# Two more outputs of the first token pair by seven products, with their weight preparation moved earlier

## The chip, the cores and the metric

One core of one Trainium2 chip runs the whole kernel. The metric is device time in microseconds (us), the median of several runs. Engines: TensorE (PE; its weight loads are PEld), VectorE (DVE), ScalarE (ACT), GpSimd (POOL) and SyncE (SP, which issues most DMAs).

## The reference, cut to what matters

```python
qn, kn = q / (norm(q, axis=1) + 1e-6), k / (norm(k, axis=1) + 1e-6)   # (6016, 256)
a = softmax(kn.T @ qn / tau)                                         # 256 x 256
x = v @ a
h = x @ w_in;  x = (h * sigmoid(1.702 * h)) @ w_out                  # 256 -> 2048 -> 256
h = x @ w2_in; y = (max(h, 0) + alpha * min(h, 0)) @ w2_out
```

All inputs are float32. The weights arrive as 64-bit numbers, read as pairs of 32-bit words.

## The kernel before

Every float32 operand is split into a high and a low part of the reduced format fp32r, and each product is three matmuls (high·high, high·low, low·high). The attention matrix is folded into the first weight, so that W1I = a · w_in is made on the chip and v goes straight into it. Tokens stand in 12 column blocks of 512 or 448, taken as six pairs per layer. The 2048 hidden channels are eight outputs j = 0 to 7 of 256.

**Two ways for one output.** `direct` takes an output's four units (a unit is 128 channels by one token block) by two products each, eight products or 24 matmuls. `quartet` takes the four units by seven products (Strassen's scheme, 21 matmuls). It needs sums of the tokens, T1 to T4, each with a high and a low part, and sums of the weights, S2 to S4 of that output. Either way the eight products `outs.next()` of the output before, with the second weight, are laid between, 24 matmuls. In the first pair of layer 1 outputs below `STRASSEN` go by `direct`, the others by `quartet`. All other pairs use `quartet` alone.

**The order of work** is written by hand, and each engine gets its instructions in the order in which the program emits them. A *place* is one call of `beside(time)`: `direct` has four an output (one a unit), the quartets of the first pair three. It counts places in `conv.now`, first emits up to `most` ScalarE steps that wait in the list `put_off`, and then VectorE steps until `time` us of stated costs are used up. The candidates are the first step of each kind in `bg` (kind 0: token sums, kind 1: weight sums) and the next step of the converter; the earliest due number goes first, and the converter wins a tie.

**The converter** turns 64-bit weights into high and low parts, one piece of 128 x 512 at a time: `ia[j]` is the inner weight of output j, `ob_[j]` the outer one. ScalarE scales (L138), VectorE does shift, power and rest (L142, L155, L158). Then a piece either takes a ScalarE copy and two more VectorE steps (less, low: L182, L185), or, where `added`, GpSimd issues an accumulating DMA (L162), three places later ScalarE's copy (L151) is asked for, and VectorE splits off the low part (L165, `settle`). The copy asked for goes through `put_off`; the split comes in the place in which the copy has been emitted. One piece in flight is asked for in a place.

**W1I.** `emit_w(j)` makes it for outputs 1 to 3; `emit_pair(j)` for outputs 4, 5 and 6, 7 with twelve matmuls of 512 columns into two PSUM banks (L723), two ScalarE writes of the high parts (L726) and two VectorE writes of the low parts (L727) right behind them. `combine` gives the weight sums S2 to S4: `whole` adds high and low again (L694), `sums_` is four small operations (L699 to L702), then ScalarE's high (L708) and VectorE's low (L705).

Of the kernel before, what the change touches and what calls it, by code (L numbers as in the profile page):

```python
# [8 lines left out]
F32 = mybir.dt.float32  # L9
# [6 lines left out]
P = 128  # L16
# [14 lines left out]
FREE = ((0.7, 2.8, 1.7), (0.0, 0.8, 0.8))  # L31
FIRST = 2.1
AHEAD = 2
QK_PARTS = [1, 3] + [4] * 9 + [2, 2, 2, 1]
TAIL = 12
LOADING = 3
LANDING = 3
STRASSEN = 6
ON_VECTOR = (4, 5, 6, 8)
# [20 lines left out]
def attention_then_two_ffns(ctx: ExitStack, tc: tile.TileContext, q, k, vT, tau, w1i, w1o, w2i, w2o, alpha, outT):  # L60
# [129 lines left out]
    class Converter:  # L190


        STEPS = (("shift", 0.45), ("power", 0.45), ("rest", 0.63), ("less", 0.63), ("low", 0.63))
        ADDED = (("shift", 0.45), ("power", 0.45), ("rest", 0.63))

# [30 lines left out]
        def time(self, piece):  # L226
            if not piece or self.landed():
                return 0.63
            return self.list(piece)[self.at][1]
# [35 lines left out]
        def step(self):  # L265

            if self.waits():
                if not self.open:
                    self.scale(True)
                scalar_work()  # L270
            if not self.next() or self.landed():
                self.settle()
                return 0.63
# [35 lines left out]
        def due(self):  # L309
            return min(x.due for x in self.left())  # L310

# [19 lines left out]
    with tc.manual_schedule():  # L331
# [26 lines left out]
        def outer(j, n=1):  # L358
            def pair():
                return tuple(WO[:, j:j + n, h].rearrange("p q a b -> p q (a b)") if n > 1 else flat(WO[:, j, h]) for h in range(2))  # L360
            return Convert(w1o[:, j * PIECE:(j + n) * PIECE].rearrange("p (a n) -> p a n", a=1), pair, added=j > 3)

# [6 lines left out]
        LAST = 4 * STRASSEN  # L369
        PAIRS = {4: 13, 6: min(21, LAST - 2)}  # L370
        for j, x in ia.items():
# [237 lines left out]

        operands, xin2, combining = {}, [], []  # L610

        class Step:
# [7 lines left out]
            def waits(self):  # L620
                return self.needs in put_off

            def run(self):
                if self.waits():
                    scalar_work()
                self.do()
                if self.then:
                    put_off.append(self.then)

        def prepare(l, p):  # L630
# [20 lines left out]
            def minus(nm, a, b):  # L651
# [4 lines left out]
                ("B11", B11), ("B21", B21), ("T1", None), ("T2", None), ("T3", None), ("T4", None), ("B22", B22))}  # L656
            D = 0.63
            early = [
# [18 lines left out]
            if (l, p) == (0, 0):  # L677
                def last():
                    ops["T4"] = operand()
                    tmp["T4"] = tmp["T2"]  # L680
                    minus("T4", B21, "T2")
                steps = [early[i] for i in (2, 3, 6, 7)] + [late[0], Step(D, None, last, hi["T4"])] + [late[i] for i in (4, 5)]
                for x, due in zip(steps, (4, 4, 4, 4, 3, 3, 3, 3)):
                    x.due = LAST - due
                return steps
            return early, late

        def combine(hi, lo, hi_s, lo_s):

            box = {}  # L690
# [12 lines left out]

            def low():
                nc.vector.tensor_tensor(lo_s(), box["s"], f32(hi_s()), ALU.subtract)  # L705

            def high():
                nc.scalar.copy(hi_s(), box["s"])  # L708

            steps = [Step(0.63, None, whole, kind=1), Step(0.9, None, sums_, high, 1), Step(0.63, high, low, kind=1)]  # L710
            combining.append(steps)
            return steps

        def combine_wi(j):
            return combine(*(WI[:, j, h, :4] for h in range(2)), *(lambda h=h: WI[:, j, h, S1:] for h in range(2)))

        def emit_pair(j):

            conv.need([ia[j], ia[j + 1]])
            for m in range(2):  # L720
# [5 lines left out]
                nc.scalar.activation(hi, src, AF.Copy, scale=rs[:, m:m + 1])  # L726
                nc.vector.scalar_tensor_tensor(lo, src, rs[:, m:m + 1], f32(hi), ALU.mult, ALU.subtract)  # L727

        def emit_w(j):
# [6 lines left out]
            for m in range(2):  # L736
                if j > 1 or m:
                    keep_hi(j, m, pw, m * C)
                    keep_lo(j, m, pw, m * C)

        bg = []
        spare = [0.0]

# [6 lines left out]
        def beside(time, convert=False, place=None, most=None):  # L750

            conv.place()
            now = scalar_work(most)
            late = now if place == 0 else []
# [18 lines left out]
        def finish(steps):  # L773

            while any(s in bg for s in steps):
                s = next(x for x in bg if x in steps) if Convert.deep else bg[0]
                bg.remove(s)
                if s.waits():
                    put_off.remove(s.needs)
                    s.needs()  # L780
# [103 lines left out]
        def direct(j, outs, mid_way):  # L884
# [3 lines left out]
            for i, (f, c) in enumerate((f, c) for f in range(2) for c in range(2)):  # L888
# [11 lines left out]
                mid_way(i)  # L900
                beside(FIRST, most=2 if (j, i) == (STRASSEN - 1, 3) else 3)
                u.low()
                units.append((f, c, u.pair))
            return Outs(0, 0, j, units)

        def quartet(l, p, j, outs, carry):
# [20 lines left out]
            ends = (l, p, j) == (1, NP - 1, NQ - 1)  # L927
            most = 1 if l else 2 if narrow else None
            u11, u22, u21, u12 = (Unit(l, 2 * j + f, c) for f, c in ((0, c0), (1, c1), (1, c0), (0, c1)))
            fork = (l, p, j) != (1, 0, 0)  # L930
            a, b = bank(), bank()
            product(a, j, A11, ops["B11"], n, True, True)
# [20 lines left out]
            if j != 1:  # L953
                beside(FREE[l][0], place=0, most=most)
            if fork:
# [11 lines left out]
            if before:  # L967
                b12.low()
            outs.next()
            product(a, j, S2, ops["T2"], n, False, True)  # L970
            u2 = copy(a)
# [5 lines left out]
            outs.next()  # L977
            beside(FREE[l][1], most=most)
            finish(late[:4])
            product(a, j, S3, ops["T3"], n, False, True)  # L980
            u3 = copy(a)
# [3 lines left out]
            evacuate()  # L985
            beside(FREE[l][2], most=most)
            finish(late)
            u22.act()
            product(a, j, A22, ops["T4"], n, False, True)
# [14 lines left out]
            return Outs(l, p, j, [(0, c0, u11.pair), (1, c1, u22.pair), (1, c0, u21.pair), (0, c1, u12.pair)])  # L1004

        operands[0, 0] = blocks
        conv.ahead = True
# [27 lines left out]
        small = [flat(G), Convert.pool.tile([P, T], F32, tag="top", name="second", bufs=3)]  # L1035
        sums0, pair1 = [], []
        outs, carry = None, []
# [21 lines left out]
        def combining_of(n):  # L1059
            combined[n] = combine_wi(n)  # L1060
            for x in combined[n]:
                x.due = LAST + 3 * ((n or NQ) - STRASSEN) - 1
            bg.extend(combined[n])

        def mid_way(i):
# [5 lines left out]
            for n, due in PAIRS.items():  # L1071
                if at == due:
                    emit_pair(n)
                    for m in (n, n + 1):
                        if m >= STRASSEN:
                            combining_of(m)
            if j == 2 and i == 0:
                nc.sync.dma_start(alpha_sb, alpha)
            if at == LAST - 10:
                sums0.extend(prepare(0, 0))  # L1080
                bg.extend(sums0)
            if at == LAST - 2:
                combining_of(0)
            next_pair()

        for j in range(NQ):
            if j:
                conv.need([ob_[j - 1]])
            if j < STRASSEN:
                outs = direct(j, outs, mid_way)  # L1090
                continue
            finish(combined[j])
            finish(sums0)
            next_pair()
# [152 lines left out]
```

## Time and profile before

| | |
|---|---|
| Median of 3 runs | 1032.64 us (1032.48 to 1032.89) |
| The profiled execution | 1033.06 us, of which the trace's span is 1031.3 us |
| TensorE busy | 1025.7 us of the span, 4634 matmuls, granted clock 1.00 |
| VectorE busy | 750.5 us (73%) |
| ScalarE busy | 758.5 us (74%) |
| GpSimd busy | 38.4 us (4%) |

The span runs from the first to the last instruction. What the profiled execution takes beyond it lies before and after. A busy share is a mean over the whole span; the first pair, which the change is about, runs from about 50 to 141 us.

### The profile page before, as it was taken

The numbers are of one execution on the slowest core, as the hardware profiler recorded it, in microseconds if no ns is written. First come the engines' busy times: TensorE is split into PE (matmuls) and PEld (weight loads), VectorE is DVE, ScalarE is ACT, GpSimd is POOL, SyncE is SP. The second block draws the span as 40 slices with busy tenths as digits, with TensorE's granted clock in tenths as the row PEclk, the third lists the DMA queues.
The fourth block names the chain that finished last, engine by engine and source line by source line (L and its number), as shares of the span: only waits on it lengthen the run. The fifth ranks groups of instructions, "written<-read, shape, count | busy, mean of one in ns | idle before, by whom it ended". The sixth has DMA issues, their size and how long they took to land.

```text
span 1031.3 us, 12536 instructions
## 1 busy us (share of the span) xinstructions
PE 1025.7 (99%) x4634; PEld 865.4 (84%) x4634; DVE 750.5 (73%) x1226; ACT 758.5 (74%) x1273; POOL 38.4 (4%) x50
## 2 busy tenths in 40 slices
PE   9999999999999999999999999999999999999998
PEld 8888888888888888888998888888888888888997
DVE  4788888877778765445637877787877787877766
ACT  6787787778778766666767777777777777867776
POOL 4401000000000000000100000000000000000000
PEclk9999999999999999999999999999999999999999
DMA  9737222224325312003553001001001000000100
GB/s 356 266 106 178 65 74 70 98 80 168 114 89 179 113 41 77 1 1 132 196 168 113 1 21 62 1 21 62 1 21 62 1 18 25 36 0 1 41 1 36
DMA packets 32445, 79.72 MB, mean 77 GB/s; under 512 B 3200, under 2 KB 7808, under 8 KB 32384
## 3 DMA queue, kind: packets, MB, share of 16 engines
q1 hardware_dynamic: 28928, 65.29, 18.3%
q0 software_dynamic: 3456, 13.63, 4.6%
q8 instruction: 36, 0.59, 0.2%
q14 instruction: 25, 0.20, 0.1%
HBM read 52.96 MB, written 23.86 MB: 74 GB/s over the span
## 4 chain that ended last, share of the span: by engine, by line
PE 99%; DMA 0%; SPq 0%; ACT 0%; issue 0%
PE ps_o L814 50%; PE ps_h L785 44%; PE gram L433 4%; PE pw L567 1%; PE pw L723 1%; DMA qk<-in_k 0%; SPq L453 0%; PE nrm L510 0%; ACT s L831 0%; PE bc L532 0%; PE pt L555 0%
## 5 line engine op out<-in xcount | busy, mean ns | idle before, releaser
L814 PE MATMUL ps_o<-ghi,wo 128*128 128x512 f32 (+1 forms) x1536 | 561.0, 385 | 0.0
L785 PE MATMUL ps_h<-x,wi 128*128 128x512 f32 (+1 forms) x2034 | 548.1, 385 | 0.0
L785 PEld LDWEIGHTS ps_h<-x,wi 128*128 128x128 f32 x2034 | 381.2, 188 | 71.9 <-DVE wi L579 0.4
L814 PEld LDWEIGHTS ps_o<-ghi,wo 128*128 128x128 f32 x1536 | 288.4, 188 | 53.7
L814 PE MATMUL ps_o<-glo,wo 128*128 128x512 f32 (+1 forms) x768 | 296.1, 386 | 0.0
L851 DVE TENSOR_TENSOR g<-ps_h,s 128x512 f32<-128x512 f32 (+1 forms) x177 | 120.1, 679 | 103.9 <-PE ps_h L785 63.5
L880 DVE SCALAR_TENSOR_TENSOR glo<-g,sign_sb,ghi 128x512 fp32r<-128x512 f32 (+1 forms) x192 | 141.5, 737 | 55.4 <-ACT ghi L874 51.0
L923 ACT COPY s<-ps_h 128x512 f32<-128x512 f32 (+1 forms) x177 | 102.2, 577 | 106.4 <-PE ps_h L785 102.2
L882 DVE TENSOR_TENSOR glo<-g,ghi 128x512 fp32r<-128x512 f32 (+1 forms) x192 | 126.4, 677 | 65.9 <-ACT ghi L876 65.1
L814 PEld LDWEIGHTS ps_o<-glo,wo 128*128 128x128 f32 x768 | 144.2, 188 | 27.2 <-DVE glo L880 0.3
L874 ACT ACTIVATE ghi<-g,sign_sb 128x512 fp32r<-128x512 f32 (+1 forms) x192 | 137.2, 714 | 16.3 <-DVE g L870 10.9
L876 ACT CAST ghi<-g 128x512 fp32r<-128x512 f32 (+1 forms) x192 | 113.1, 612 | 3.4
L862 ACT ACTIVATE g<-ps_h 128x512 f32<-128x512 f32 (+1 forms) x108 | 63.3, 586 | 41.6 <-PE ps_h L785 41.1
L866 ACT ACTIVATE g<-g,sign_sb 128x512 f32<-128x512 f32 (+1 forms) x97 | 69.4, 716 | 29.2 <-DVE g L851 28.7
L870 DVE SCALAR_TENSOR_TENSOR g<-g,slope_sb 128x512 f32<-128x512 f32 (+1 forms) x97 | 71.6, 738 | 16.7 <-ACT g L866 16.6
L870 DVE SCALAR_TENSOR_TENSOR g<-ps_h,slope_sb,g 128x512 f32<-128x512 f32 (+1 forms) x95 | 69.7, 734 | 0.0
L934 ACT COPY ps_h<-ps_h 128x512 f32<-128x512 f32 (+1 forms) x89 | 50.2, 564 | 26.4 <-PE ps_h L785 26.1
L866 ACT ACTIVATE g<-ps_h,sign_sb 128x512 f32<-128x512 f32 (+1 forms) x95 | 64.3, 676 | 1.9 <-PE ps_h L785 0.2
L862 ACT ACTIVATE g<-g 128x512 f32<-128x512 f32 (+1 forms) x84 | 52.3, 622 | 13.8 <-DVE g L851 13.3
L433 PE MATMUL gram<-qk 128*128 128x256 f32 x156 | 34.3, 380 | 1.0 <-DMA qk<-in_k 1.0
L433 PEld LDWEIGHTS gram<-qk 128*128 128x128 f32 x156 | 29.4, 190 | 5.2 <-issue 1.4
L649 DVE TENSOR_TENSOR x<-t,x 128x512 fp32r<-128x512 f32 (+1 forms) x48 | 32.0, 674 | 0.0
(123 smaller groups left out, 493.5 us busy)
## 6 DMA issues: line engine op xcount, KB each, us to landing
wi<-w2i POOLq DMA_DIRECT2D x8, 896.0 KB, 4.9
xraw<-in_vT SPq DMA_DIRECT2D x10, 512.0 KB, 5.5
x<-ob SPq DMA_DIRECT2D x20, 256.0 KB, 2.9
xraw<-x SPq DMA_DIRECT2D x10, 512.0 KB, 3.7
out_T<-ob SPq DMA_DIRECT2D x20, 256.0 KB, 2.0
qk<-in_q SPq DMA_DIRECT2D x9, 512.0 KB, 10.3
qk<-in_k SPq DMA_DIRECT2D x9, 512.0 KB, 10.6
raw<-in_w1i SPq DMA_DIRECT2D x8, 512.0 KB, 5.0
```

The lines of the kernel that those rows point to most:

```text
L433: nc.tensor.matmul(gram[m][:, :C], tiles[i][:, 1, r, m * P:(m + 1) * P], tiles[i][:, 0, r, :], start=(t == 0), stop=(t == R - 1))
L785: nc.tensor.matmul(ps[:, :n], WI[:, wq, a, blk], x[:, b, :n], start=(start and i == 0), stop=(stop and i == 2), skip_group_check=True)
L814: nc.tensor.matmul(acc_ps[c][d][:, :n], WO[:, j, a, f, d * P:(d + 1) * P], (hi, lo)[b][:, :n], start=(start and i == 0), stop=(stop and i ...
L851: nc.vector.tensor_tensor(self.src, ps[:, :self.n], s[:, :self.n], ALU.add)
L862: nc.scalar.activation(self.g, self.src, AF.Gelu_apprx_sigmoid)
L866: nc.scalar.activation(self.g, self.src, AF.Copy, scale=sign_sb[:, self.f])
L870: nc.vector.scalar_tensor_tensor(self.g, self.src, slope_sb[:, self.f], self.g, ALU.mult, ALU.max)
L874: nc.scalar.activation(self.hi, self.g, AF.Copy, scale=sign_sb[:, self.f])
L876: nc.scalar.copy(self.hi, self.g)
L880: nc.vector.scalar_tensor_tensor(self.lo, self.g, sign_sb[:, self.f], f32(self.hi), ALU.mult, ALU.subtract)
L882: nc.vector.tensor_tensor(self.lo, self.g, f32(self.hi), ALU.subtract)
L923: nc.scalar.copy(s[:, :n], ps[:, :n])
```

## The change

`STRASSEN` goes from 6 to 4, so outputs 4 and 5 of the first pair go by `quartet` too. W1I for outputs 4 and 5 is made in place 12 in place of 13, for 6 and 7 in place 17, which is now the first place of output 4's quartet, in place of 21. The low parts of such a pair are emitted behind the VectorE steps of the place (`settle_w`). For outputs 4 to 7, ScalarE writes a whole copy of W1I out of PSUM, put off to the next place, and `combine` uses it in place of VectorE's `whole`. Outer pieces 2 and 3 go by the accumulating DMA. T1 to T4 are prepared from place 7 on and finished inside output 4's quartet, each before the product that reads it. The weight sums' high parts are put off one place more (`aging`). Budgets of places and stated costs change a little. The sums of outputs 4 and 5 were made in the second pair before.

```diff
+MORE = (0, 1), (1, 1), (2, 1)
-STRASSEN = 6
+SETTLING = 1
+STRASSEN = 4
...
-        STEPS = (("shift", 0.45), ("power", 0.45), ("rest", 0.63), ("less", 0.63), ("low", 0.63))
+        STEPS = (("shift", 0.45), ("power", 0.45), ("rest", 0.62), ("less", 0.62), ("low", 0.62))
...
-            return min(x.due for x in self.left())
+            return min(x.due - (0 if x in self.flying else 4 if x.added else 1) for x in self.left())
...
-            return Convert(w1o[:, j * PIECE:(j + n) * PIECE].rearrange("p (a n) -> p a n", a=1), pair, added=j > 3)
+            return Convert(w1o[:, j * PIECE:(j + n) * PIECE].rearrange("p (a n) -> p a n", a=1), pair, added=j >= 2)
...
-        PAIRS = {4: 13, 6: min(21, LAST - 2)}
+        PAIRS = {4: 12, 6: 17}
...
-                for x, due in zip(steps, (4, 4, 4, 4, 3, 3, 3, 3)):
-                    x.due = LAST - due
+                for x, due in zip(steps, (-1, 0, -1, 0, 1, 1, 1, 1)):
+                    x.due = LAST + due
...
-            steps = [Step(0.63, None, whole, kind=1), Step(0.9, None, sums_, high, 1), Step(0.63, high, low, kind=1)]
+            steps = ([] if t else [Step(0.62, None, whole, kind=1)]) + [Step(0.9, t and t[1], sums_, high, 1), Step(0.62, high, low, kind=1)]
...
-                nc.vector.scalar_tensor_tensor(lo, src, rs[:, m:m + 1], f32(hi), ALU.mult, ALU.subtract)
+                lows.append(lambda hi=hi, lo=lo, src=src, m=m: nc.vector.scalar_tensor_tensor(
+                    lo, src, rs[:, m:m + 1], f32(hi), ALU.mult, ALU.subtract))
...
+                full = lambda part=part, src=src, m=m: nc.scalar.activation(part, src, AF.Copy, scale=rs[:, m:m + 1])
+                copies.append(full)
...
+        def settle_w():
+
+            for do in lows:
+                do()
+            lows.clear()
+            put_off.extend(copies)
+            copies.clear()
+            for n in sums_next:
+                combining_of(n)
+            sums_next.clear()
...
-                beside(FIRST, most=2 if (j, i) == (STRASSEN - 1, 3) else 3)
+                beside(FIRST + (0.5 if (j, i) in MORE else 1.0 if lows else 0), most=2 if (j, i) == (STRASSEN - 1, 3) else 3)
+                settle_w()
...
+        def operands_of(which):
+
+            finish([x for i, x in enumerate(sums0) if (0, 1, 0, 1, 2, 3, 2, 3)[i] <= which])
...
+            free = (0.9, 3.1, 2.1) if narrow and j < NQ - 1 else FREE[l]
...
+            if narrow:
+                pairs(conv.now)
             outs.next()
+            if narrow:
+                operands_of(1)
             product(a, j, S2, ops["T2"], n, False, True)
...
-            beside(FREE[l][1], most=most)
+            beside(free[1] + (1.0 if lows else 0), most=most)
+            if narrow:
+                settle_w()
             finish(late[:4])
+            if narrow:
+                operands_of(2)
             product(a, j, S3, ops["T3"], n, False, True)
...
+            if narrow:
+                operands_of(3)
             u22.act()
             product(a, j, A22, ops["T4"], n, False, True)
```

## Rows read from the trace of the kernel before

**Rows 1.** The page, part 4: shares of the chain that ended last.

```profile
PE 99%; DMA 0%; SPq 0%; ACT 0%; issue 0%
```

**Rows 2.** Waits of TensorE: line and releaser; total us, times, longest.

```profile
PE gram L433 <- DMA qk<-in_k: 1.0, 1, 1.0
```

**Rows 3.** Stretches: us, then busy us of PE, PEld, DVE, ACT, POOL; clock; DMA.

```profile
68.10:100.90 32.80, 32.80 (x151) 27.36 (x151) 27.18 (x51) 23.80 (x42) 4.77 (x6) 1.00 0.67 168
...
120.90:131.10 10.20, 10.20 (x47) 8.45 (x46) 9.16 (x20) 9.10 (x18) 0.88 (x1) 1.00 0.16 28
...
141.30:1031.30 890.00, 886.46 (x3985) 747.62 (x3983) 642.95 (x1032) 656.77 (x1114) 8.53 (x16) 1.00 0.18 61
```

**Rows 4.** Timeline of TensorE: start, us, line, what, count.

```profile
88.21 0.62 PE L723 MATMUL pw<-wi_hi,eT_hi 128*128 128x512 f32 x2
...
90.94 0.85 PE L785 MATMUL ps_h<-x,wi 128*128 128x512 f32 x3
...
96.38 0.84 PE L785 MATMUL ps_h<-x,wi 128*128 128x512 f32 x3
...
130.40 1.52 PE L785 MATMUL ps_h<-x,wi 128*128 128x512 f32 x6
...
140.60 1.52 PE L785 MATMUL ps_h<-x,wi 128*128 128x512 f32 x6
```

**Rows 5.** Timeline of VectorE: start, us, line, what; in brackets idle time before.

```profile
91.86 0.75 DVE L727 SCALAR_TENSOR_TENSOR wi<-pw,rs,wi 128x512 fp32r<-128x512 f32 x1 [0.62 <-ACT wi L726]
92.53 0.68 DVE L158 SCALAR_TENSOR_TENSOR p<-raw,p 128x512 f32<-128x512 uint32 x1
...
98.78 0.43 DVE L142 TENSOR_SCALAR top<-p 128x512 uint32<-128x512 uint32 x1 [1.64 <-ACT p L138]
99.24 0.43 DVE L155 TENSOR_SCALAR p<-top 128x512 uint32<-128x512 uint32 x1
...
100.31 0.69 DVE L882 TENSOR_TENSOR glo<-g,ghi 128x512 fp32r<-128x512 f32 x1
...
101.52 1.29 DVE L649 TENSOR_TENSOR x<-t,x 128x512 fp32r<-128x512 f32 x2
102.72 0.69 DVE L882 TENSOR_TENSOR glo<-g,ghi 128x512 fp32r<-128x512 f32 x1
...
117.87 0.29 DVE L699 TENSOR_TENSOR s<-t 128x128 f32<-128x128 f32 x1
...
118.81 0.69 DVE L882 TENSOR_TENSOR glo<-g,ghi 128x512 fp32r<-128x512 f32 x1
```

**Rows 6.** Timeline of ScalarE, same columns.

```profile
91.14 0.69 ACT L726 ACTIVATE wi<-pw,rs 128x512 fp32r<-128x512 f32 x1 [0.68 <-PE pw L723]
91.72 0.65 ACT L138 ACTIVATE p<-raw 128x512 f32<-128x512 f32 x1
...
97.06 1.14 ACT L645 CAST x<-t 128x512 fp32r<-128x512 f32 x2
98.10 0.65 ACT L138 ACTIVATE p<-raw 128x512 f32<-128x512 f32 x1
98.66 0.58 ACT L862 ACTIVATE g<-ps_h 128x512 f32<-128x512 f32 x1
99.27 0.62 ACT L876 CAST ghi<-g 128x512 fp32r<-128x512 f32 x1
99.80 0.62 ACT L151 CAST wo<-p 128x512 fp32r<-128x512 f32 x1
```

**Rows 7.** Waits between 50 and 141 us, columns as in Rows 2.

```profile
ACT wi L575 <- DVE wi L579: 1.4, 2, 0.8
...
ACT wi_hi L151 <- DMA p<-top: 0.9, 1, 0.9
```

**Rows 8.** The tile p, 50 to 130 us: GpSimd's issues (ns, min/median/max), landing.

```profile
L162 POOL DMA_DIRECT2D p<-top x8: 853/870/1147, 76.0 to 122.1; - x8
...
DMA to landing us min/median/max: 3.3/4.9/6.8
```

More of the change, by code (lines that the diff above doesn't have):

```diff
@@ L190, in attention_then_two_ffns @@
     class Converter:
-        STEPS = (("shift", 0.45), ("power", 0.45), ("rest", 0.63), ("less", 0.63), ("low", 0.63))
-        ADDED = (("shift", 0.45), ("power", 0.45), ("rest", 0.63))
+        STEPS = (("shift", 0.45), ("power", 0.45), ("rest", 0.62), ("less", 0.62), ("low", 0.62))
+        ADDED = (("shift", 0.45), ("power", 0.45), ("rest", 0.62))
         def __init__(self):
@@ L227, in time @@
             if not piece or self.landed():
-                return 0.63
+                return 0.62
             return self.list(piece)[self.at][1]
@@ L272, in step @@
                 self.settle()
-                return 0.63
+                return 0.62
             if not self.open:
@@ L608, in attention_then_two_ffns @@
         conv.steps(2)
-        operands, xin2, combining = {}, [], []
+        operands, xin2, combining, aging = {}, [], [], []
         class Step:
@@ L620, in waits @@
             def waits(self):
-                return self.needs in put_off
+                return self.needs in put_off or any(self.needs is x for _, x in aging)
             def run(self):
@@ L626, in run @@
                 self.do()
-                if self.then:
+                if self.then and self.kind and conv.ahead and Convert.deep:
+                    aging.append((conv.now, self.then))
+                elif self.then:
                     put_off.append(self.then)
@@ L656, in prepare @@
                 ("B11", B11), ("B21", B21), ("T1", None), ("T2", None), ("T3", None), ("T4", None), ("B22", B22))}
-            D = 0.63
+            D = 0.62
             early = [
@@ L682, in prepare, with combine @@
                 steps = [early[i] for i in (2, 3, 6, 7)] + [late[0], Step(D, None, last, hi["T4"])] + [late[i] for i in (4, 5)]
-                for x, due in zip(steps, (4, 4, 4, 4, 3, 3, 3, 3)):
-                    x.due = LAST - due
+                for x, due in zip(steps, (-1, 0, -1, 0, 1, 1, 1, 1)):
+                    x.due = LAST + due
                 return steps
             return early, late
-        def combine(hi, lo, hi_s, lo_s):
-            box = {}
+        def combine(hi, lo, hi_s, lo_s, t=None):
+            box = {"t": t and t[0]}
             def whole():
@@ L714, in combine_wi @@
         def combine_wi(j):
-            return combine(*(WI[:, j, h, :4] for h in range(2)), *(lambda h=h: WI[:, j, h, S1:] for h in range(2)))
+            return combine(*(WI[:, j, h, :4] for h in range(2)), *(lambda h=h: WI[:, j, h, S1:] for h in range(2)), wholes.get(j) if j >= STRASSEN else None)
+        lows, copies, wholes = [], [], {}
         def emit_pair(j):
@@ L726, in emit_pair @@
                 nc.scalar.activation(hi, src, AF.Copy, scale=rs[:, m:m + 1])
-                nc.vector.scalar_tensor_tensor(lo, src, rs[:, m:m + 1], f32(hi), ALU.mult, ALU.subtract)
+                lows.append(lambda hi=hi, lo=lo, src=src, m=m: nc.vector.scalar_tensor_tensor(
+                    lo, src, rs[:, m:m + 1], f32(hi), ALU.mult, ALU.subtract))
+                if j + 1 < STRASSEN:
+                    continue
+                if not m:
+                    both = xin[1].tile([P, 2, 4, P], F32, tag=f"x{7 + j // 2}", name="whole")
+                part = both[:, :, 2 * m:2 * m + 2]
+                full = lambda part=part, src=src, m=m: nc.scalar.activation(part, src, AF.Copy, scale=rs[:, m:m + 1])
+                copies.append(full)
+                if m:
+                    wholes[j], wholes[j + 1] = (both[:, 0], full), (both[:, 1], full)
         def emit_w(j):
@@ L739, in emit_w @@
                     keep_lo(j, m, pw, m * C)
+        def settle_w():
[7 more added lines that the diff above has]
+            sums_next.clear()
         bg = []
+        sums_next = []
         spare = [0.0]
@@ L752, in beside @@
             conv.place()
+            while aging and conv.now - aging[0][0] >= SETTLING:
+                put_off.append(aging.pop(0)[1])
             now = scalar_work(most)
@@ L778, in finish @@
                 if s.waits():
-                    put_off.remove(s.needs)
+                    aged = [x for x in aging if x[1] is s.needs]
+                    if aged:
+                        aging.remove(aged[0])
+                    else:
+                        put_off.remove(s.needs)
                     s.needs()
@@ L928, in quartet @@
             most = 1 if l else 2 if narrow else None
+            free = (0.9, 3.1, 2.1) if narrow and j < NQ - 1 else FREE[l]
             u11, u22, u21, u12 = (Unit(l, 2 * j + f, c) for f, c in ((0, c0), (1, c1), (1, c0), (0, c1)))
             fork = (l, p, j) != (1, 0, 0)
+            if narrow:
+                operands_of(0)
             a, b = bank(), bank()
@@ L953, in quartet @@
             if j != 1:
-                beside(FREE[l][0], place=0, most=most)
+                beside(free[0], place=0, most=most)
             if fork:
@@ L985, in quartet @@
             evacuate()
-            beside(FREE[l][2], most=most)
+            beside(free[2], most=most)
             finish(late)
+            if narrow:
+                operands_of(3)
             u22.act()
@@ L1004, in quartet @@
             return Outs(l, p, j, [(0, c0, u11.pair), (1, c1, u22.pair), (1, c0, u21.pair), (0, c1, u12.pair)])
+        sums0 = []
         operands[0, 0] = blocks
@@ L1035, in attention_then_two_ffns @@
         small = [flat(G), Convert.pool.tile([P, T], F32, tag="top", name="second", bufs=3)]
-        sums0, pair1 = [], []
+        pair1 = []
         outs, carry = None, []
@@ L1061, in combining_of, with pairs @@
             for x in combined[n]:
-                x.due = LAST + 3 * ((n or NQ) - STRASSEN) - 1
+                x.due = LAST + 3 * ((n or NQ) - STRASSEN) - 3
             bg.extend(combined[n])
+        def pairs(at):
+            for n, due in PAIRS.items():
+                if at == due:
+                    emit_pair(n)
+                    sums_next.extend(m for m in (n, n + 1) if m >= STRASSEN)
+            if at == max(LAST - 1, PAIRS[6]):
+                sums_next.append(0)
         def mid_way(i):
@@ L1070, in mid_way @@
                 emit_w(j + 1)
[L1071 to L1076, printed above, removed]
+                if j + 1 >= STRASSEN:
+                    sums_next.append(j + 1)
+            pairs(at)
             if j == 2 and i == 0:
                 nc.sync.dma_start(alpha_sb, alpha)
-            if at == LAST - 10:
+            if at == 7:
                 sums0.extend(prepare(0, 0))
                 bg.extend(sums0)
-            if at == LAST - 2:
-                combining_of(0)
             next_pair()
@@ L1091, in attention_then_two_ffns @@
                 continue
+            assert not lows and not sums_next and not copies
             finish(combined[j])
-            finish(sums0)
             next_pair()
```

## The prediction

> **What bounds the kernel now.** I read the shares of the chain that ended last first: TensorE holds 99% of it [rows 1]. Next, its waits: from 2 us on it is held by one DMA, for 1.0 us at the very start [rows 2], and the table of stretches shows it busy all of the time from 68.1 to 100.9 and from 120.9 to 131.1 us, at clock 1.00 [rows 3]. So in the first pair every matmul added or saved counts in full, as long as nothing else makes TensorE wait. Its timeline gives the price: a quartet's 45 matmuls take 140.60 - 130.40 = 10.20 us, 0.2267 us each, and two units of `direct`, 24 matmuls, take 96.38 - 90.94 = 5.44 us [rows 4].
>
> VectorE's timeline must be read against this one. It is no bound by its mean, but from 68.1 to 100.9 us it is busy 27.18 of 32.80 us [rows 3], and it runs behind: the low part of the last unit before 96.38 us begins at 100.31 [rows 4, 5]. TensorE doesn't feel it, because a unit's parts are read only one output later.
>
> **What TensorE saves.** Outputs 4 and 5 lose one product of three matmuls each: 6 x 0.2267 = 1.36 us. The twelve matmuls of each W1I pair only move. The Trainium skill, "TensorE: Matmul & The Clock Gate", section on the back-to-back issue gap, gives 512 columns as N/2.4 + 2.5 ns, 215.8 ns; by it the saving would be an estimated 1.29 us. The row's 226.7 ns differs from it, and I keep the row's.
>
> **What the other engines get.** VectorE gets two sums of PSUM with a copy in each of two more quartets (4 x 0.60 us; two operations take 102.72 - 101.52 = 1.20 [rows 5]), and the weight sums of outputs 4 and 5 from the second pair, 0.94 for the four small ones (117.87 to 118.81) and 0.60 for the low part, 3.1 in all. It loses `whole` for outputs 6 and 7 and one step in each of outer pieces 2 and 3, 2.4. ScalarE gets three copies in each new quartet and two highs of sums at about 0.52, and four whole copies at 0.58 (91.14 to 91.72, casts from 97.06 [rows 6]): 6.5 us. The second pair loses two weight sums; as all that follows 141.3 us has TensorE busy 886.46 of 890 us with VectorE at 642.95 [rows 3], neither this nor the finer 0.62 budgets there (a third place now holds 0.62 + 0.62 + 0.45) is worth anything, either way; its cover is VectorE's 28% of idle time, and a late step there would cost its own 0.60. The whole copies take the pool's last two token slots, which the second pair's tokens take only after the sums.
>
> So in sum VectorE has only 3.1 us more. What matters is when. T1 to T4, the sums of output 4 and the pieces of outputs 6 and 7 are now due in or before output 4's quartet, which starts at 96.38 us as output 4 did before [rows 4], and there a step is read by TensorE in the same output.
>
> **The order, by the code's own rules.** Outer piece 3 gets its third step in place 9 (budget 2.6: a split 0.62, that step 0.62, two steps of 0.45), flies three places, and so ScalarE's copy of it is asked for in place 12. That is the place of the pair's twelve matmuls. They start at 85.48 now, one unit of 2.72 us before 88.21 [rows 4]. ScalarE's second high part came 91.14 - 88.21 = 2.93 us after the start [rows 4, 6], so 88.41. Queued behind it stand T1's high, a scaling and only then the copy: 88.41 + 0.58 + 0.52 + 0.56 = 90.07, and 0.62 for itself, 90.69. VectorE's first step of place 12 is the split that needs it. Going through the places from 67 us on by the same rules I find it free at about 88.5 (an estimate), so it loses some 2 us; but whatever it did before, it starts again at 90.7. From there it has, with no wait at all, in this order:
>
> - place 12: that split 0.60, three steps of outer piece 4 1.53 (98.78 to 100.31), T2 0.60, the pair's two lows 1.34 (91.86 to 92.53 each [rows 5]), the unit's low 0.60: 95.39
> - place 13: sums of output 4 0.94, T1's low and the unit's low 1.20: 97.53
> - place 14: the sums' low, T2's low, a split, the unit's low 2.40: 99.93
> - place 15: sums of output 5 0.94, the split of inner piece 7 0.60, a shift 0.46 (98.78 to 99.24), the unit's low 0.60: 102.53
> - output 4: T3, a unit's low, a sums' low, T4, T3's low 3.00: 105.53; a split 0.60, power and rest 1.07, a shift 0.46, the lows of the second pair 1.34, the sum u22 0.60, T4's low 0.60: 110.20
>
> TensorE wants T4's low in the 50th matmul of output 4 (36 of products and outputs and the pair's 12 stand before its product, whose second matmul reads the low part): 96.38 + 49 x 0.2267 = 107.49. **Lower bound of the stall: 110.20 - 107.49 = 2.7 us.** VectorE would have to reach output 4 by 102.53 - 2.7 = 99.8 us, earlier than the 100.9 it reaches with less work before.
>
> The upper bound adds ScalarE, whose instructions also wait in line. T2's high waits for VectorE's T2 until 93.45. The whole copies wait for the lows on the same bank, as ScalarE's second W1I write waits for VectorE's low in the trace, 1.4 us in two waits [rows 7]: the second one is out at 95.4. Behind it stand two units' activations (0.61) and highs (0.53), a scaling, three casts: 4.4 us [rows 6], and then the copy that seeds the third product, done at 100.35, where TensorE wants it at 99.10. The pair's third matmul then waits for inner piece 7 until 102.2 (VectorE itself lost 0.7 to the sums), and S2's product ends at 102.2 + 16 x 0.2267 = 105.8. Its copy precedes the sums' high of output 5 on ScalarE: 105.8 + 0.2 + 0.55 + 0.52 = 107.1. VectorE's sums' low waits for this high, with T4 and T3's low queued behind: 107.1 + 1.80 + 4.67 = 113.6. **Upper bound: 113.6 - 107.5 = 6.1 us.** I take the middle, 4.4, since the second chain needs every landing in time and some of its links may fall out.
>
> After this, VectorE waits for TensorE again and the lag is gone; in outputs 5 to 7 the budgets and the six own operations make 6.1 + 3.6 = 9.7 of 10.2 us, tight but covered. The lag is paid once.
>
> **Sum.** The profiled execution took 1033.06 us, span 1031.3 and 1.76 around it: 1033.06 - 1.36 + 4.4 = 1036.1. It stood 0.42 above the median of the runs, 1032.64; against this median the forecast is 1035.7, and the bounds give 1034.0 to 1037.4. A measurement of this kernel tells about 0.2% from no change, 2.07 us: under 1030.57 is faster, above 1034.71 slower.
>
> **Rivals.**
>
> *No stall (not slower).* VectorE reaches output 4 by 99.8. That needs 2.7 us less waiting than I count; the wait in place 12 is 2 of these and the sums' wait 0.7. For it: in the trace TensorE waits for nothing though VectorE is 4.5 us behind at 96.38 [rows 4, 5]. Against: there only whole outputs hang on it. Then 1032.64 - 1.36 = 1031.3, no change by the bound above.
>
> *A part of it.* One link is out of place by a step or two and the stall is 1 to 2.7 us: 1032.3 to 1034.0.
>
> *Landings decide.* Ten accumulating DMAs in place of eight, seven of them within places 5 to 12. ScalarE waited 0.9 us for one [rows 7], with landings of 3.3 to 6.8 us [rows 8]. One landing on the chain at 6.8 instead of the median 4.9 holds ScalarE, and all queued behind it, 1.9 us longer: 1035.7 + 1.9 = 1037.6 or more. [...]
>
> *More than the matmuls.* A gain over 2.07 us would need TensorE time that isn't there [rows 2, 3].
>
> **How the numbers follow.** The forecast gets 0.56: each link is a rule of the code and a row, but there are some forty in line. Of this, 0.12 lies at stalls under 1.36 + 2.07 = 3.43 us, so within the bound. No stall gets 0.26, a part 0.10, landings 0.06, more than the matmuls 0.02. Slower is 0.44 + 0.06 = 0.50, no change 0.12 + 0.26 + 0.10 = 0.48, faster 0.02. The likeliest case's own range is 1034.0 to 1037.4; as cases on both sides of the bound hold much, the whole range runs from no stall, 1031.2, to 1037.4.
>
> **What would show it.** TensorE's waits between 99 and 112 us: in the second matmul of T4's product on VectorE's L649, in the third one of the second pair on L165, in the third product on ScalarE's copy (the line of L934). On VectorE, an idle time of about 2 us in the split before W1I's pair at 90 us, and the low part of the last `direct` unit near 102.5 to 103.2. If that low part stands before 100 us, or the split isn't in place 12, I am wrong, and the time is near 1031.3; if TensorE waits in outputs 5 to 7 too, the lag isn't paid once. A quartet of output 5 longer than 10.2 us would show that.

## The result and the profile after

The kernel takes 1040.47 us after the change, the median of six runs (1039.88 to 1042.05), against 1032.63 for six of the kernel before: ratio 1.0078, 95% interval 1.0068 to 1.0089. It is slower by 7.8 us. The forecast was 1035.7, its range ended at 1037.4. One of the four runs of experiment 1 took 5948.7 us and is left out of every figure below.

In the new kernel the lines have moved: products are L819 (L785 before), outputs L848 (L814), W1I's pair L729 (L723), its high and low writes L732 and L733, the whole copies L740, the tokens' high and low L649 and L653, the sums' high and low L712 and L709, the copy that seeds a product L976, a piece's scaling L140, its copy L153 and split L167.

The waits of TensorE answer to [rows 2], where there was one DMA (each row: line, releaser, total us, times, longest):

```profile
PE ps_h L819 <- DVE x L653: 3.0, 2, 2.1
PE ps_o L848 <- ACT wo L153: 1.1, 1, 1.1
...
PE pw L729 <- DVE wi_lo L167: 0.5, 1, 0.5
PE ps_h L819 <- ACT wi L712: 0.5, 1, 0.5
```

All of these, and three of 0.2 to 0.4 us more, lie in the first pair. The table of stretches shows where (columns as in [rows 3]): TensorE, without a gap there before, loses half of the stretch from 110 to 115 us.

```profile
105.00:110.00 5.00, 4.39 (x19) 3.05 (x17) 1.97 (x5) 2.82 (x5) 0.00 (x0) 1.00 0.37 105
110.00:115.00 5.00, 2.43 (x9) 1.61 (x9) 4.96 (x10) 2.23 (x4) 0.88 (x1) 1.00 0.49 131
115.00:120.00 5.00, 4.82 (x21) 4.00 (x22) 3.22 (x7) 3.76 (x8) 0.87 (x1) 1.00 0.47 80
```

TensorE's timeline gives the prices (start, us, line, in brackets the idle time before and what ended it):

```profile
82.08 0.84 PE L819 MATMUL ps_h<-x,wi 128*128 128x512 f32 x3
84.02 0.50 PE L848 MATMUL ps_o<-ghi,wo 128*128 128x512 f32 x1 [1.10 <-ACT wo L153]
...
86.64 0.62 PE L729 MATMUL pw<-wi_hi,eT_hi 128*128 128x512 f32 x2
...
97.54 0.84 PE L819 MATMUL ps_h<-x,wi 128*128 128x512 f32 x3
...
99.53 1.23 PE L819 MATMUL ps_h<-x,wi 128*128 128x512 f32 x3 [0.47 <-ACT wi L712]
...
101.68 0.97 PE L819 MATMUL ps_h<-x,wi 128*128 128x512 f32 x3 [0.23 <-ACT ps_h L976]
...
103.59 0.73 PE L729 MATMUL pw<-wi_lo,eT_hi 128*128 128x512 f32 x2 [0.48 <-DVE wi_lo L167]
...
109.25 0.49 PE L819 MATMUL ps_h<-x,wi 128*128 128x512 f32 x1 [0.35 <-ACT x L649]
110.67 0.73 PE L819 MATMUL ps_h<-x,wi 128*128 128x512 f32 x2 [0.92 <-DVE x L653]
...
115.18 0.73 PE L819 MATMUL ps_h<-x,wi 128*128 128x512 f32 x2 [2.08 <-DVE x L653]
...
116.44 1.54 PE L819 MATMUL ps_h<-x,wi 128*128 128x512 f32 x6
...
126.66 1.52 PE L819 MATMUL ps_h<-x,wi 128*128 128x512 f32 x6
```

Two places lose time. From 82.08 to 86.64 us stand 12 matmuls, 2.72 us of work in 4.56: **1.84 us, on the second weight of output 2** (outer piece 2). From 97.54 to output 5's first product, three matmuls into the group at 116.44, so 117.12, stand 57 matmuls (45 and the pair's 12), 12.92 us of work in 19.58: **6.66 us, in output 4**. The bracketed idle times of output 4 add up to only 4.53. The rest is refilling, some 0.35 us for each of the six waits: three products take 0.84 us at 97.54, but 1.23 and 0.97 behind a wait (99.53, 101.68), and the idle time counts only from the end of the matmul before, which otherwise overlaps the next one's start. Output 5 then takes 126.66 - 116.44 = 10.22 us, as a quartet did before [rows 4].

The spans differ by 1038.1 - 1031.3 = 6.8: + 1.84 + 6.66 - 1.36 of matmuls - 0.69 of a shorter start (the kernel before had waited 1.0 us there [rows 2], so everything below stands 0.69 earlier in this trace than in that one) + 0.35 that is left. Nearly all of this rest, 0.29, lies at one place of a later pair: matmul for matmul from the end, the offset between the two traces grows there from 6.46 to 6.75. The first of six matmuls starts right behind a folding on VectorE, and the six take 1.66 us in place of 1.52:

```profile
290.04 1.66 PE L819 MATMUL ps_h<-x,wi 128*128 128x512 f32 x6
```

```profile
289.30 0.68 DVE L885 TENSOR_TENSOR g<-ps_h,s 128x512 f32<-128x512 f32 x1
```

The traces of experiments 1 to 8 lose the same there, those of the kernel before and of experiment 9 do not.

Why output 4 waits stands on ScalarE and VectorE. First VectorE, around places 12 and 15:

```profile
91.87 0.69 DVE L167 TENSOR_TENSOR wo<-p,wo 128x512 fp32r<-128x512 f32 x1 [3.19 <-ACT wo L153]
...
104.39 0.68 DVE L657 TENSOR_TENSOR t<-xraw 128x512 f32<-128x512 f32 x1
...
108.71 0.69 DVE L709 TENSOR_TENSOR wi<-s,wi 128x512 fp32r<-128x512 f32 x1 [3.03 <-ACT wi L712]
109.32 0.69 DVE L657 TENSOR_TENSOR t<-xraw,t 128x512 f32<-128x512 f32 x1
...
113.85 0.68 DVE L885 TENSOR_TENSOR g<-ps_h,second 128x512 f32<-128x512 f32 x1
114.45 0.68 DVE L653 TENSOR_TENSOR x<-t,x 128x512 fp32r<-128x512 f32 x1
```

and ScalarE in the same time:

```profile
89.57 0.69 ACT L732 ACTIVATE wi<-pw,rs 128x512 fp32r<-128x512 f32 x1 [0.68 <-PE pw L729]
...
91.23 0.60 ACT L153 CAST wo<-p 128x512 fp32r<-128x512 f32 x1
...
107.58 0.59 ACT L959 COPY G<-ps_h 128x512 f32<-128x512 f32 x1 [0.68 <-PE ps_h L819]
108.06 0.62 ACT L712 CAST wi<-s 128x512 fp32r<-128x512 f32 x1
108.58 0.62 ACT L649 CAST x<-t 128x512 fp32r<-128x512 f32 x1
```

The last chain is read from the bottom. TensorE waits for T4's low part (VectorE, 114.45). That stands behind VectorE's list from 108.71 on, and VectorE could not begin it because its next instruction, the low part of output 5's sums, needs ScalarE's high part at 108.06; this one was long possible, but stands on ScalarE behind a copy (107.58) of a product that TensorE itself made late. TensorE waits, through two queues, for itself. This is read from one trace; experiments 3 and 5 to 7 test it.

### The profile page after: what moved, and what is told of

Read it like the earlier page. It is cut to its first block, busy times and chain, and to the rows that moved or that the text cites. A ratio compares the mean times of both kernels' runs of the same rounds, so it can differ in the third digit from the quotient of the medians.

```text
span 1038.1 us, 12543 instructions
## 1 busy us (share of the span) xinstructions
PE 1027.6 (99%) x4628; PEld 863.8 (83%) x4628; DVE 748.5 (72%) x1224; ACT 764.1 (74%) x1283; POOL 40.2 (4%) x52
## 4 chain that ended last, share of the span: by engine, by line
PE 97%; DVE 2%; ACT 1%; issue 0%; POOL 0%; POOLq 0%
PE ps_o L848 48%; PE ps_h L819 43%; PE gram L435 4%; PE pw L569 1%; PE pw L729 1%; PE idle L393 0%; DVE p L160 0%; DVE wo L167 0%; DVE x L653 0%; DVE glo L916 0%; ACT p L140 0%; DVE wi L733 0%; ACT whole L740 0%; DVE wi_lo L167 0%; DVE t L657 0%
## 5 line engine op out<-in xcount | busy, mean ns | idle before, releaser
L848 PE MATMUL ps_o<-ghi,wo 128*128 128x512 f32 (+1 forms) x1536 | 560.6, 385 | 1.3 <-ACT wo L153 1.1
L819 PE MATMUL ps_h<-x,wi 128*128 128x512 f32 (+1 forms) x2028 | 547.6, 386 | 4.1 <-DVE x L653 3.0
L819 PEld LDWEIGHTS ps_h<-x,wi 128*128 128x128 f32 x2028 | 379.7, 188 | 78.2 <-DVE x L653 3.6
L848 PEld LDWEIGHTS ps_o<-ghi,wo 128*128 128x128 f32 x1536 | 288.4, 188 | 55.8 <-ACT wo L153 1.5
L848 PE MATMUL ps_o<-glo,wo 128*128 128x512 f32 (+1 forms) x768 | 296.1, 386 | 0.0
L885 DVE TENSOR_TENSOR g<-ps_h,s 128x512 f32<-128x512 f32 (+1 forms) x177 | 120.1, 678 | 108.0 <-PE ps_h L819 63.1
L848 PEld LDWEIGHTS ps_o<-glo,wo 128*128 128x128 f32 x768 | 144.2, 188 | 27.2 <-DVE glo L914 0.3
L896 ACT ACTIVATE g<-ps_h 128x512 f32<-128x512 f32 (+1 forms) x104 | 60.7, 584 | 29.5 <-PE ps_h L819 28.4
L976 ACT COPY ps_h<-ps_h 128x512 f32<-128x512 f32 (+1 forms) x91 | 51.2, 563 | 27.7 <-PE ps_h L819 27.2
L896 ACT ACTIVATE g<-g 128x512 f32<-128x512 f32 (+1 forms) x88 | 54.8, 623 | 16.5 <-DVE g L885 16.0
L653 DVE TENSOR_TENSOR x<-t,x 128x512 fp32r<-128x512 f32 (+1 forms) x48 | 32.2, 673 | 0.0
```

The source lines that it names most:

```text
L819: nc.tensor.matmul(ps[:, :n], WI[:, wq, a, blk], x[:, b, :n], start=(start and i == 0), stop=(stop and i == 2), skip_group_check=True)
L848: nc.tensor.matmul(acc_ps[c][d][:, :n], WO[:, j, a, f, d * P:(d + 1) * P], (hi, lo)[b][:, :n], start=(start and i == 0), stop=(stop and i ...
L885: nc.vector.tensor_tensor(self.src, ps[:, :self.n], s[:, :self.n], ALU.add)
L896: nc.scalar.activation(self.g, self.src, AF.Gelu_apprx_sigmoid)
```

## The experiments

Seven edits, alone and combined, in nine kernels. The kernel before, run on the same chips, stood at 1032.70 us beside experiments 1 to 4, at 1032.82 beside 5, 6 and 9, and at 1032.72 beside 7 and 8.

**1. Outer pieces 2 and 3 without the DMA, as before the change.**

```
-            return Convert(w1o[...], pair, added=j >= 2)
+            return Convert(w1o[...], pair, added=j > 3)
```

> Outer pieces 2 and 3 back on the VectorE route, all else as changed. The theory says that the changed kernel's lateness has two parts: 1.84 us because the second weight of output 2 comes too late by the accumulating DMA, and 6.66 us in output 4, where VectorE and ScalarE deliver T3, T4 and the sums late. Here the first part goes at once, and so does VectorE's idle time of 3.19 us in the split of outer piece 3 at 88.6 us, against 1.2 us more of VectorE work: about 1037.4 us in place of 1040.4. The rival, that VectorE simply has too much work before output 4 and its idle times are only the other side of that, says that the 1.2 us are added to the second part: 1040.4 - 1.8 + 1.2 = 1039.8.

Measured: 1042.90 us (1042.32 to 1043.61, three runs), ratio 1.0097 (1.0077 to 1.0117), worse than both expectations. Neither piece is waited for any more, but VectorE's extra steps come back as longer waits in output 4 and a new one in output 5. Its waits of TensorE:

```profile
PE ps_h L819 <- DVE x L653: 3.2, 1, 3.2
PE ps_h L819 <- ACT whole L740: 1.9, 1, 1.9
PE ps_h L819 <- ACT wi L712: 1.8, 1, 1.8
```

So this part of the change is not the cause of output 4's stall: without it output 4 waits longer. How much undoing it costs is less clear. All three runs had a mean clock of 0.998 or 0.997 (0.81 and 0.85 in the stretches 110 to 115 and 115 to 120 us of the trace, on which more below); against the two runs of the changed kernel at 0.998, 1042.0, it is 0.9 us. The edit also changes the order of the pieces, since `due` puts an `added` piece four places ahead and another only one.

**2. ScalarE's copy of outer piece 3 ahead of W1I's pair.**

```
+            if at == PAIRS[4]:
+                conv.ask()
+                scalar_work()
             pairs(at)
```

> ScalarE's copy of outer piece 3 and T1's high are emitted ahead of the first W1I pair in place 12, not behind ScalarE's two writes of the pair; VectorE's order is the same. Theory: the split starts near 89.2 instead of 91.87, the scaling of outer piece 4 then holds VectorE until 90.9, and VectorE gains about 1.6 us, which come off the waits of TensorE between 98 and 104 us and carry through: about 1038.8 us. Rival, that the sums' high of output 5 on ScalarE sets T3's and T4's lows whatever comes before: no change, 1040.4.

Measured: 1039.68 us (1038.92 to 1040.43), ratio 1.0065 (1.0050 to 1.0080). The split of place 12 stands at 89.51 with 0.61 us of idle time before, where it was 3.19, and TensorE's waits for the sums and for the third product's seed are gone. The waits for tokens remain, and so does the one for outer piece 2 (0.9):

```profile
PE ps_h L819 <- DVE x L653: 3.0, 2, 2.1
```

So place 12 was worth about 1 us, not the stall: 0.8 by the medians, whose intervals overlap those of the changed kernel, and 1.2 between the runs of both kernels at a clock of 0.999 or more.

**3. The sums' high parts given to ScalarE at once** (no `aging`).

```
-                if self.then and self.kind and conv.ahead and Convert.deep:
-                    aging.append((conv.now, self.then))
-                elif self.then:
+                if self.then:
```

> The weight sums' high parts go into the list of ScalarE's steps at once, not one place later. The high of output 5's sums then goes out in output 4's first place, before the copy of S2's product. Theory: VectorE's idle time of 3.03 us before that sums' low part goes, but T3's high, which still stands behind the same copy, holds the next step: a gain of 1.2 us, 1039.2. Rival, that this wait alone is what makes T3 and T4 late: the full 3.0 us, 1037.4.

Measured: 1040.79 us (1039.86 to 1042.08), ratio 1.0077 (1.0062 to 1.0092): nothing gained, neither theory right. VectorE's wait moved on from 108.71 by two instructions, from the sums' low part to T3's, whose high part now stood behind ScalarE's copies:

```profile
106.41 0.69 DVE L707 TENSOR_TENSOR wi<-s,wi 128x512 fp32r<-128x512 f32 x1
...
109.88 0.69 DVE L651 TENSOR_TENSOR x<-t,x 128x512 fp32r<-128x512 f32 x1 [2.17 <-ACT x L647]
```

**4. Outer piece 2 due earlier** (`ob_[2].due = 11` in place of 12), which puts its steps ahead of inner pieces.

> Outer piece 2 goes ahead of inner pieces 4 and 5 in the converter's order, so that its copy and split come two places earlier; only these pieces swap places on VectorE and ScalarE. Theory: TensorE's waits for it near 84 us, 1.84 us with the restarts, are gone, and all behind them, which hangs on TensorE through the first W1I pair, moves forward as a whole: 1038.6 us. Rival, that VectorE's work is the limit from 68 us on and the first wait only hides a part of the second: the waits in output 4 grow by what is saved, 1040.2 or more.

Measured: 1039.62 us (1038.66 to 1040.36), ratio 1.0064 (1.0049 to 1.0079). The wait for outer piece 2 is gone, and all those of output 4 stay. Two runs took 1038.66 and 1038.97, as expected, two 1040.27 and 1040.36; the granted clock tells them apart (last section).

**5. T3 and T4 due two places earlier.** This is the test of the chain above: their highs should then stand on ScalarE ahead of the second pair's.

```
-                for x, due in zip(steps, (-1, 0, -1, 0, 1, 1, 1, 1)):
+                for x, due in zip(steps, (-3, -2, -3, -2, -1, -1, -1, -1)):
```

> The two token differences of output 4's third and fourth products, with their high and low halves, become due two places earlier, and nothing else is changed. Theory (ScalarE's queue: the third difference's high half stands behind the copies that wait for the pair's first product, and VectorE idles 3.03 us behind the sums' high half): both high halves are made ahead of the second pair's high halves, TensorE's three waits for x (0.35, 0.92 and 2.08 us, each with about 0.27 us of refilling) go, 4.2 us: 1035.7 us. The waits for the sums and for the third product's seed (0.47, 0.23, 0.48) stay, and so does outer piece 2's. Rival (VectorE simply has more work than time in places 12 to 15): what is moved forward pushes the sums' low half back, the same time is lost at other waits: 1039.0 to 1040.5 us.

Measured: 1037.32 us (1037.01 to 1039.23), ratio 1.0042 (1.0025 to 1.0059). The three waits for x are gone, with the same amount of work on every engine (VectorE is busy 748.7 us, 748.5 before the edit). ScalarE makes both highs at once, 102.34, and VectorE both lows, 105.57:

```profile
102.34 1.22 ACT L649 CAST x<-t 128x512 fp32r<-128x512 f32 x2 [1.01 <-DVE t L657]
```

```profile
105.57 1.29 DVE L653 TENSOR_TENSOR x<-t,x 128x512 fp32r<-128x512 f32 x2
109.24 0.69 DVE L709 TENSOR_TENSOR wi<-s,wi 128x512 fp32r<-128x512 f32 x1 [2.38 <-ACT wi L712]
...
113.30 0.68 DVE L885 TENSOR_TENSOR g<-ps_h,second 128x512 f32<-128x512 f32 x1
```

The rival of too much work is refuted as it was stated: the median isn't in its 1039.0 to 1040.5, and the one run that is, 1039.23, has a clock of 0.998 (last section). But the gain is 3 us and not the 4.2 of the theory, since a part comes back at other waits. VectorE still waits 2.38 us for the sums' high part, and now the first folding of output 4's products (L885) is late behind it, 1.77 us of TensorE's time. Outer piece 2 is waited for 1.7 us in place of 1.1, inner piece 7 0.8 in place of 0.5.

**6. Edits 2 to 5 together.**

> The same, with outer piece 2 due earlier, outer piece 3's copy ahead of the pair's high halves and the sums' high halves given to ScalarE at once. Theory: the gains add, about 4.2 for the tokens, 1.1 for outer piece 2 and 1.0 for the copy: 1033.6 us, between 1033.0 and 1034.5, still over the kernel before because the sums' low half and the pair's second weight halves come late. Rival (VectorE's work): no better than 1037 us. If every wait of output 4 went, 1031.3 us.

Measured: 1035.11 us (1034.55 to 1035.59, ten runs), ratio 1.0023 (1.0013 to 1.0032), in no run a lower mean clock than 0.999. The gain is 5.4 us, which the four edits' own gains allow (4.5 in sum by the medians, 6.0 at a clock of 0.999 or more); the time is 0.6 us above the theory's range. The rival, no better than 1037, is refuted. What is left of TensorE's waits, beside 0.2 us for a seed:

```profile
PE ps_h L818 <- DVE g L884: 1.2, 1, 1.2
...
PE pw L728 <- DVE wi_lo L167: 0.8, 1, 0.8
```

**7. The same without edit 3.**

> The same three edits as in the kernel of 1035.1 us (tokens earlier, outer piece 2 earlier, the copy ahead), without the sums' high halves given to ScalarE at once. Theory (with the tokens out of the way, the sums' high half of output 5 costs nothing on TensorE's path): same time, 1034.8 to 1035.5 us. Rival (that high half behind the outer piece's copy pushes VectorE's low half, the steps behind it and so the fold back by the copy's 0.53 us): 1035.5 to 1036.0 us.

Measured: 1036.15 us (1035.69 to 1036.18), ratio 1.0032 (1.0019 to 1.0045). The rival has the mechanism, and the time is 0.15 us above its range: the wait for the folding is 2.3 us in place of 1.2. ScalarE makes the sums' high part behind the outer piece's copy (0.52), and that copy itself had waited 0.44 us for a landing, which the rival didn't count.

```profile
PE ps_h L820 <- DVE g L886: 2.3, 1, 2.3
```

So edit 3, worth nothing alone, is worth 1.0 us once the tokens are out of its way.

**8. The kernel of experiment 6, and outer pieces 4 to 7 due one place later** (`ob_[j].due += 1`).

> The kernel with the tokens earlier, outer piece 2 earlier, the copy ahead and the sums' high halves at once (1035.1 us), and outer pieces 4 to 7 due one place later, which moves conversion steps of theirs from ahead of to behind the work of output 4 on VectorE. Theory (the 1.20 us wait for the first folding of output 4 stands behind conversion steps on VectorE, and 1.5 us of steps go ahead of the second pair's low halves into VectorE's wait for ScalarE): the wait for the fold and its refilling go, 1.45 us, the second pair's wait for inner piece 7 grows by about 0.65: 1034.3 us. Rival (the fold waits for TensorE's own products or for the pair's high halves): no change, 1034.8 to 1035.5 us.

Measured: 1038.66 us (1038.40 to 1038.97), ratio 1.0059 (1.0042 to 1.0075). A miss, by 4.4 us. The folding no longer holds output 4: VectorE reaches it and waits itself 1.65 us for ScalarE's copy. But the new due times reordered ScalarE's list as well (the highs of T3 and T4 now stand ahead of the third product's seed), and TensorE waits 1.0 us for that seed, 1.0 for inner piece 7, 1.1 for a whole copy and, in a later output, 0.5 for a folding:

```profile
PE ps_h L820 <- ACT whole L741: 1.1, 1, 1.1
...
PE pw L730 <- DVE wi_lo L167: 1.0, 1, 1.0
```

**9. Seven products for outputs 5 to 7 only** (`STRASSEN = 5`), with edits 2 and 4.

> Seven products for outputs 5, 6 and 7 alone, output 4 directly, with outer piece 2 due earlier and the copy ahead: four more places lie between the weights and the first product by seven, and half as much TensorE time is saved again (three matmuls of 0.2267 us, 0.68 us). Theory (the lead in places decides): no wait at the first product, 1031.9 us, under the kernel before. Rival (the work is too much for VectorE and ScalarE however it is placed): waits stay, 1034 us or more.

Measured: 1032.45 us (1032.03 to 1033.44, ten runs), ratio 0.9997 (0.9988 to 1.0006). In the first pair TensorE waits for nothing:

```profile
105.00:120.00 15.00, 15.00 (x67) 12.37 (x67) 14.32 (x30) 11.95 (x23) 1.73 (x2) 1.00 0.41 103
```

VectorE is far fuller from 105 to 120 us, 14.32 us of 15, than in the changed kernel, 1.97 + 4.96 + 3.22 = 10.15, so a nearly full VectorE doesn't by itself make TensorE wait. With four more places ahead of the first quartet nothing is late; but this kernel also has one quartet less to prepare, and no run tells the two apart. It beats the changed kernel by 8 us and equals the one before: 0.37 us between the medians is under what a measurement tells. It is 0.55 over what I expected, and 0.31 over 1032.82 - 0.68, the kernel before on the same chip less the matmuls saved; the interval of the ratio covers that.

## Why the prediction was wrong, point by point

**The miss in terms of the sum.** The median is 1040.47 - 1035.7 = 4.77 us above the forecast. Of this, 6.66 - 4.4 = 2.26 are the stall of output 4 and 1.84 is outer piece 2, which the sum put at nothing; the shorter start takes off 0.69, the rest adds 0.35. The last 1.01 lies in the profiled executions: the one before stood 0.42 above its median, the one after 0.59 below. Two steps failed, then. The stall as the mean of its bounds was too small, but even its upper bound, 6.1, gives only 1037.4; of the 3.07 us beyond that, outer piece 2 is the largest part.

**What TensorE saves: right.** The products' group has six matmuls fewer, 2028 (2034 before), and all its idle time is in the first pair:

```profile
L819 PE MATMUL ps_h<-x,wi 128*128 128x512 f32 (+1 forms) x2028 | 547.6, 386 | 4.1 <-DVE x L653 3.0
```

**The order in places 12 to 15: right.** The split of place 12 began 91.87 - 89.57 = 2.30 us after ScalarE's second high part; 90.7 - 88.41 = 2.3 was worked out. From there VectorE reached output 4's list, the first T3 step, in 104.39 - 91.87 = 12.52 us; the working has 102.53 - 90.7 = 11.8 and leaves out two short waits for ScalarE (0.16 and 0.52). VectorE's idle time before the split was 3.19 us and not some 2, because outer piece 2's wait had moved the pair back but not VectorE's own list.

**"I take the middle, 4.4": the first step that failed.** The upper bound's chain, through ScalarE's seed copy, inner piece 7, the copy of S2's product and the sums' high part, ran link by link: the sums' high part ended at 108.68 against 107.1 + 1.16 = 108.3 (the pair began 1.16 us later than in the working: 1.84 less 0.69), T4's low part at 115.1 against 113.6 + 1.16 = 114.8. The stall was 6.66 against 6.1. Two bounds that are two chains over the same instructions aren't ends of an unknown cost: the instruction waits for the later one. The three waits named as what would show it are there, each on the instruction named; the other three of output 4 (0.47, 0.35, 0.92) stand on the same two queues and were not named. "Some of its links may fall out" had no row behind it. Experiments 5 to 7 show the chain to be the cause of the waits for tokens: with the tokens moved off it, these go. Experiment 6 leaves 2.2 us of waits that have other readers, the folding and inner piece 7 first.

**Outer piece 2, put at nothing: the second step that failed.** I followed outer piece 3 through its DMA, ScalarE's copy and the split, and counted piece 2 only among the landings. It takes the same way, and its reader, output 2's first `outs`, comes at 82.8 us. ScalarE's timeline shows the copy last of three, one asked for in a place, at 83.36:

```profile
76.82 0.62 ACT L153 CAST wi_hi<-p 128x512 fp32r<-128x512 f32 x1 [1.34 <-PE pw L569]
...
80.93 0.60 ACT L153 CAST wi_hi<-p 128x512 fp32r<-128x512 f32 x1
...
83.36 0.61 ACT L153 CAST wo<-p 128x512 fp32r<-128x512 f32 x1
```

Its landing was the longest of the nine between 50 and 125 us, 6.7 us (the median is 5.4), but over at 82.34, 1.02 us ahead of the copy. So the queue of copies made it late, and without it the landing alone would have left little room. Edit 4 moves the piece forward in that queue, and the wait of 1.84 us is gone.

**The second pair and what follows, put at nothing either way: nearly right.** The one place at 290.04 costs 0.29 us. Which part of the change makes VectorE's folding late there was not tried.

**The sum with both terms as measured:** 1033.06 - 1.36 + 6.66 + 1.84 - 0.69 + 0.35 = 1039.86, the profiled execution (1039.88). It closes because the 0.35 is what was left of the spans. The median is 0.6 higher, in part by the clock (below): without the two runs at 0.998 the mean of the others is 1040.3.

**The lag is paid once: right.** Output 5 took 10.22 us, and TensorE's waits end at 115.18.

**The rivals.** *No stall*, given 0.26, rested on the trace of before, in which VectorE ran 4.5 us behind without harm. That trace couldn't speak for an output that reads its own token sums. *Landings*: in output 4 of the changed kernel no engine waited for one; in experiment 7 one held ScalarE for 0.44 us.

## What to carry to other kernels

When a change moves work to just ahead of its reader, write down for each moved piece the time at which it is read and the last instruction that makes it, for every piece and not for the one that looks worst. With engines that take their work in order, follow the queue of each engine that the chain passes through and take the latest chain; a mean between chains is no estimate. And look for loops in which the late engine feeds a queue that it waits for: there the order of a few instructions may be worth 3 us with the amount of work unchanged (experiment 5), while a step's due time (experiment 8) may reorder another engine's queue.

## What the runs showed of the hardware that I had not expected

A stall of TensorE may cost more than its length. In the run of edit 4, TensorE works from 110 to 112 us, is idle for nearly all of 112 to 114 (0.04 us busy), works again, and then the granted clock falls to half, 1.2 GHz, and is back at 1.00, 2.4 GHz, from 119 us on (the clock stands just ahead of the last two numbers, the DMA's share and GB/s):

```profile
110.00:112.00 2.00, 1.87 (x8) 1.12 (x6) 1.97 (x5) 1.11 (x2) 0.29 (x1) 1.00 0.74 247
112.00:114.00 2.00, 0.04 (x1) 0.04 (x1) 2.00 (x5) 1.32 (x2) 0.58 (x1) 1.00 0.48 85
114.00:115.00 1.00, 1.00 (x4) 0.82 (x5) 0.93 (x2) 0.26 (x1) 0.00 (x0) 1.00 0.58 98
115.00:116.00 1.00, 1.00 (x4) 0.79 (x3) 0.00 (x0) 1.00 (x3) 0.39 (x1) 0.55 0.00 0
116.00:117.00 1.00, 1.00 (x3) 0.78 (x3) 0.13 (x1) 0.36 (x1) 0.48 (x1) 0.50 0.00 0
117.00:118.00 1.00, 1.00 (x4) 0.76 (x3) 1.00 (x2) 0.00 (x0) 0.00 (x0) 0.50 1.08 188
118.00:119.00 1.00, 1.00 (x5) 0.83 (x4) 0.76 (x2) 0.85 (x2) 0.00 (x0) 0.74 0.44 74
```

It costs 0.45 + 0.50 + 0.50 + 0.26 = 1.7 us. The traces of experiments 1, 2 and 5 have such a fall too, to the same 0.50 and at the same cost of 1.7 us, though the waits just ahead of it differ (3.16, 2.1 and 1.77 us). The profiled execution of the changed kernel has the same wait, 2.08 us, and its clock stays at 1.00. Two of that kernel's six runs had a mean clock of 0.998 and took 1042.0 us, four had 0.999 or 1.00 and took 1039.9 to 1040.6; of edit 4's four runs the two with 0.998 are the slower ones, by 1.5 us. The Trainium skill, "TensorE: Matmul & The Clock Gate", section on what's actually happening, says that the clock follows how busy TensorE has lately been. The traces agree: each of the four falls stands behind a stall. But a stall doesn't always bring it. Experiment 7's one long wait, 2.27 us, lies between these in length, and in none of its five runs was the mean clock under 0.999; nor was it in experiments 6 (ten runs, waits up to 1.2 us), 8 (four, up to 1.1) and 9 (ten, none). Runs under 0.999 were two of six of the changed kernel, all three of experiment 1, two of four each in 2, 3 and 4, and one of four in 5. What decides between two executions of the same stall, no run here shows. The forecast had no such term.
